# Two waiting lines for a sparse-attention and soft-MoE kernel's loads, and a step's second transposes ahead of its values

## The chip, the cores and the metric

The kernel runs on one core of one Trainium2 chip. The metric is the device time of one execution in microseconds. In the texts PE is the matrix engine (TensorE), PEld its weight loads, DVE the vector engine, ACT the scalar engine, POOL GpSimd, and SP the engine whose queue issues every DMA of this kernel.

## What is computed

The input is a batch of 8 with 8 heads of width 64, 512 local positions and 32 global ones. Everything is float32.

```python
s_g = scale * np.matmul(q_g, k_all.transpose(0, 1, 3, 2))      # 32 global queries see all 544 keys
out_g = np.matmul(sm(s_g), v_all)
s_ll = np.where(np.abs(pos[:, None] - pos[None, :]) <= 32, s_ll, -1e9)   # a local query: 65 neighbours
s_l = np.concatenate([s_lg, s_ll], axis=-1)                    # and the 32 global keys
out_l = np.matmul(sm(s_l), v_all)
x = concatenate([out_g, out_l]) laid out as (4352, 512)
logits = x @ phi                                               # 32 slots: 8 experts of 4
slot_input = softmax_over_rows(logits).T @ x
slot_out[e] = np.maximum(slot_input[e] @ w1[e], 0) @ w2[e]     # w1 512 x 1024, w2 1024 x 512
out = softmax_over_slots(logits) @ slot_out
```

## The kernel before

**Attention.** A unit u is four heads of one batch element, 16 units in all; it has three loads: k (704 KB), q (544 KB) and v (780 KB). Each unit is worked in two steps, so k counts 32 steps, with u = k // 2. The loop at L591 writes, for each step, in this order: the transposes of the shifted scores of step k-1 and their exponentials (transpose_exp, tiles t and pt), the parts run(k, "t"), the global queries of the next unit (make_qg, POOL, which reads the next q), the shift of the global scores (tile spg, POOL), the values of step k-2 (tile o), in odd steps the global values (tile og), the parts run(k, "b"), in even steps the transposes of the global scores (global_transpose, tile tg, exponential into ptg), the parts run(k, "c"), and then the scores of step k+1 (masks and scores, tile s, which read k and q) and their maximum and shift on DVE (tiles mx and sp). An even step closes with the global scores of its unit (tile g, copied into spg by ACT). make_v then copies pieces of v into va and vb on POOL, four copies a step, because the values read their windows of 128 keys from them.

The parts in "t", "b" and "c" are the first half of the mixture: "c" holds transposes of finished rows x (tile xt, in odd steps), "b" the logits (pl) and slot sums (pa), "t" the transposes of the exponentials (ptl).

**Order.** From L548 on the order of PE, DVE, ACT, POOL and SP is the order in which the code writes the work (manual_schedule), so each engine works through its own list, and an instruction that waits holds up those behind it. Transposes take one PSUM bank each from a ring of four (function bank): a group can start when the group four places before it has been read. The tiles o, g and the first scores share one other pair of banks (psV).

**Loads.** All loads go through SP's queue in order. The weights of the experts come in 64 pages of 512 KB (w); 30 of them have a place of their own and are loaded during the attention, two each unit. Four more take the places of the last k and q tiles. The rest follow when attention's buffers are given up (from L716 on). The loads of the attention are paced: matmul and transpose are wrapped (counted, L145) and count PE's instructions, and after every 253.75 of them release (L157) takes loads from the head of the list line, as long as the head fits in what is left of 10700 bytes a partition (GROUP; k takes 5632, q 4352, v 6240, a page 4096), and makes each wait for the PE instruction just written. need issues from the list without that wait, when a load that is needed next has not been issued. At the end of an even step the loop appends a page, k and q of unit u+2, and another page; v of unit u+1 goes to the head of the list in the odd step. The first loads (L538 to L546) and v of unit 1 are not paced.

## Time and profile before

| what | value |
|---|---|
| runs of the kernel before | 287.5 us median of 3 (286.36 to 287.97) |
| the profiled execution | 288.08 us, of it the span 286.3 us |
| mean granted clock of PE in it | 0.973 |
| DMA traffic | 77.05 MB, mean 269 GB/s |

The profile is of one execution. A row of its timeline gives the start in us from the span's start, the length, the engine, the line of the code, the operation, and output<-input by the names of the tiles; in brackets stands the idle time of the engine before it and who ended it. The chain of waits goes back from the last instruction to whatever released each step. "issue" as a releaser means that an engine waited for nothing that the profile shows. Line numbers are those of the kernel before; those of the changed kernel are larger by 1 to 5.

### The profile page before, as it was taken

The page shows a single profiled execution, that of the slowest core. Times are in us where ns is not written, and L with a number is a line of the kernel's source. Part 1 is how long each engine was busy: PE and PEld are TensorE (multiplying, and loading weights), DVE is VectorE, ACT ScalarE, POOL GpSimd, SP SyncE. Part 2 cuts the span into 40 slices and gives each one's busy share as a digit, 9 for nine tenths or more (in the row PEclk, how much of TensorE's full clock was granted, in tenths as well). Part 3 has the DMA queues.
Part 4 walks back from the last instruction along what each step waited for, and adds up shares of the span by engine and source line. Part 5 has one row for each costly group of instructions (what it writes and reads, how often), then busy time and mean ns, then how long its engine had stood idle before and what let it go on. Part 6 is the DMA issues. An engine that isn't in the chain of part 4 may idle for free.

```text
span 286.3 us, 14380 instructions
## 1 busy us (share of the span) xinstructions
PE 251.2 (88%) x6472; PEld 177.8 (62%) x6472; DVE 169.1 (59%) x360; ACT 120.9 (42%) x298; POOL 123.1 (43%) x182
## 2 busy tenths in 40 slices
PE   7749999899899986898999999899987999999920
PEld 4437777677677774676777877777765433655510
DVE  0744857576687856185678678577635764133730
ACT  1213464445546353344544555545473212124520
POOL 1077649557566673636465666466720000000000
PEclk9997999999999999799999999999999999999985
DMA  6964886867868875567576776878887999959998
GB/s 209 368 239 151 252 285 208 290 241 254 267 223 275 298 242 204 185 252 265 191 265 218 252 294 214 250 259 279 293 293 273 417 374 410 406 195 307 287 308 274
DMA packets 26909, 77.05 MB, mean 269 GB/s; under 512 B 2528, under 2 KB 12768, under 8 KB 26848
## 3 DMA queue, kind: packets, MB, share of 16 engines
q1 hardware_dynamic: 26848, 76.13, 76.2%
q8 instruction: 51, 0.84, 1.2%
q14 instruction: 10, 0.08, 0.1%
HBM read 67.21 MB, written 8.91 MB: 266 GB/s over the span
## 4 chain that ended last, share of the span: by engine, by line
PE 66%; DMA 15%; DVE 4%; issue 4%; SPq 2%; ACT 2%; POOL 2%; DVEq 0%; ACTq 0%; POOLq 0%
PE s L147 14%; DMA q<-in_qT_dram 12%; PE o L147 9%; PE t L147 8%; PE po L820 5%; PE g L147 5%; PE xt L147 4%; PE tg L147 4%; DMA v<-in_vS_dram 3%; PE pc L854 3%; PE pa L147 3%; PE ph L655 3%; PE pl L147 2%; PE og L147 2%; PE ht L670 1%
## 5 line engine op out<-in xcount | busy, mean ns | idle before, releaser
L261 DVE TENSOR_REDUCE mx<-s 128x8 f32<-128x1024 f32 x32 | 39.2, 1225 | 56.8 <-PE s L147 56.8
L147 PE MATMUL s<-k,q 64*32 64x128 f32 x2048 | 40.0, 281 | 9.0 <-DMA q<-in_qT_dram 4.8
L147 PEld LDWEIGHTS s<-k,q 64*32 64x32 f32 x2048 | 30.2, 108 | 21.3 <-issue 18.8
L272 ACT ACTIVATE pt<-t 128x512 f32<-128x512 f32 x64 | 34.9, 601 | 13.1 <-PE t L147 12.8
L263 DVE TENSOR_TENSOR sp<-s,mx 128x1024 f32<-128x1024 f32 x32 | 39.2, 1224 | 1.1
L215 POOL COPY va<-v 128x520 f32<-128x520 f32 (+1 forms) x32 | 23.2, 725 | 37.1 <-DMA v<-in_vS_dram 26.2
L147 PE MATMUL o<-v,pt 128*32 128x65 f32 x768 | 36.4, 221 | 1.7 <-issue 1.7
L147 PE MATMUL o<-va,pt 128*32 128x65 f32 x768 | 36.4, 221 | 0.2 <-POOL va L216 0.2
L147 PE MATMUL o<-vb,pt 128*32 128x65 f32 x512 | 35.3, 221 | 1.0 <-POOL vb L218 1.0
L147 PE MATMUL t<-con,sp 128*128 128x128 f32 x256 | 35.0, 280 | 0.0
L147 PEld LDWEIGHTS o<-v,pt 128*32 128x32 f32 x768 | 30.6, 109 | 4.7 <-issue 4.7
L147 PEld LDWEIGHTS o<-va,pt 128*32 128x32 f32 x768 | 30.6, 109 | 3.1 <-issue 2.2
L321 POOL TENSOR_SCALAR spg<-spg,m 128x640 f32<-128x640 f32 x16 | 30.1, 1883 | 2.0 <-DVE m L320 0.5
L147 PEld LDWEIGHTS o<-vb,pt 128*32 128x32 f32 x512 | 29.9, 110 | 1.2 <-POOL vb L218 1.2
L147 PEld LDWEIGHTS t<-con,sp 128*128 128x128 f32 x256 | 27.4, 141 | 5.1 <-issue 2.8
L384 ACT COPY xT<-xt 128x512 f32<-128x512 f32 x31 | 16.8, 588 | 32.2 <-PE xt L147 32.2
L316 ACT COPY spg<-g 128x640 f32<-128x640 f32 x16 | 11.1, 696 | 35.3 <-PE g L147 35.3
L224 POOL COPY qg<-q 64x64 f32<-64x64 f32 x32 | 7.4, 232 | 41.4 <-DMA q<-in_qT_dram 34.3
L297 DVE TENSOR_TENSOR xh<-o,r 128x256 f32<-128x256 f32 x64 | 24.2, 419 | 1.1
L216 POOL COPY va<-v 32x520 f32<-32x520 f32 (+1 forms) x32 | 23.0, 719 | 2.0
L147 PE MATMUL g<-k,qg 128*64 128x512 f32 (+2 forms) x192 | 21.8, 362 | 0.0
L346 ACT ACTIVATE xg<-og,rg 32x64 f32<-32x64 f32 x64 | 19.6, 306 | 4.6 <-DVE rg L342 1.9
(143 smaller groups left out, 399.1 us busy)
## 6 DMA issues: line engine op xcount, KB each, us to landing
w<-in_w_dram SPq DMA_DIRECT2D x64, 512.0 KB, 5.8
v<-in_vS_dram SPq DMA_DIRECT2D x16, 780.0 KB, 4.7
k<-in_kT_dram SPq DMA_DIRECT2D x15, 704.0 KB, 4.8
out_dram<-ob SPq DMA_DIRECT2D x32, 256.0 KB, 3.2
q<-in_qT_dram SPq DMA_DIRECT2D x15, 544.0 KB, 5.9
out_dram<-ob SPq DMA_DIRECT2D x8, 64.0 KB, 2.0
k<-in_kT_dram SPq DMA_DIRECT2D x1, 416.0 KB, 4.0
q<-in_qT_dram SPq DMA_DIRECT2D x1, 288.0 KB, 4.0
```

The costliest lines, as they stand in the source:

```text
L147: ins = emit(*args, **kw)
L215: nc.gpsimd.tensor_copy(va, v[:, m0:m1])
L216: nc.gpsimd.tensor_copy(va[0:32], v[0:32, m0 + 1:m1 + 1])
L261: nc.vector.tensor_reduce(mx, ps, axis=AX.X, op=ALU.max, negate=True)
L263: nc.vector.tensor_tensor(sps[k], ps, bc(mx, P), ALU.add)
L272: nc.scalar.activation(e[:, hh], pt, AF.Exp, scale=SCALE)
L297: nc.vector.tensor_tensor(xhs[u][:, 2 * a + t, :].rearrange("p (h d) -> p h d", h=4), po[:, t, :, 0:D], bc(r[:, t, :], D), ALU.mult)
L316: nc.scalar.copy(spg, pg[:, 0:640])
L321: later["shift"] = lambda: nc.gpsimd.tensor_scalar(spg, spg, m1, None, ALU.add)
L346: nc.scalar.mul(xgs[u // NU2][p0:p0 + 32, 256 * g + D * j:256 * g + D * j + D], po[32 * j:32 * j + 32, 0:D], r[32 * j:32 * j + 32])
L384: nc.scalar.copy(xT, pt)
L820: nc.tensor.matmul(po[h][32 * j:32 * j + 32, :], hTs[r][:, f, 32 * j:32 * j + 32], wt[1, 4 * r + j, h, f // 4][:, 256 * (f % 4):256 * (f % ...
```

## The change

Four things are done.

1. There are two lists. k, q and v stay in line, the pages go to fillers. release fills its room from line first, and from fillers with what is left. Both pages of a unit are appended at the end of the even step. What is left in fillers after the loop is issued there.
2. v of units 0 and 1 is no longer issued among the first loads: both wait in line and are released by PE's count.
3. In step 0 the two vb copies are made by ACT and not by POOL, and the shift of the first global scores is written ahead of make_v.
4. global_transpose and run(k, "c") stand right behind run(k, "t"), ahead of make_qg, of the shift and of the values.

```diff
--- before.py
+++ after.py
@@ -140,7 +140,7 @@
 
 
     count = [0, FIRST_BLOCK]
-    line = []
+    line, fillers = [], []
 
     def counted(emit, n):
         def f(*args, **kw):
@@ -156,16 +156,17 @@
 
     def release(ins):
         room = GROUP
-        while line and line[0][1] <= room:
-            room -= line[0][1]
-            issue(ins)
+        for q in (line, fillers):
+            while q and q[0][1] <= room:
+                room -= q[0][1]
+                issue(ins, q)
 
     def pace(load, ins):
         tc.add_manual_dep(load.ins, ins.ins.name,
                           mybir.DependencyInfo(mybir.DependencyClass.Sync, mybir.DependencyReason.DATA), reason="paced")
 
-    def issue(ins=None):
-        load = line.pop(0)[0]()
+    def issue(ins=None, q=None):
+        load = (line if q is None else q).pop(0)[0]()
         if ins is not None:
             pace(load, ins)
 
@@ -180,7 +181,7 @@
             resident[0] += 1
             return load_slot(resident[0] - 1)
 
-        line.append((load, 4096))
+        fillers.append((load, 4096))
 
     ks, qs, vs = {}, {}, {}
 
@@ -214,8 +215,9 @@
         vb = at.tile([P, 2, 4, VD], F32, tag=f"vb{a}", name=f"vb{k}")
         nc.gpsimd.tensor_copy(va, v[:, m0:m1])
         nc.gpsimd.tensor_copy(va[0:32], v[0:32, m0 + 1:m1 + 1])
-        nc.gpsimd.tensor_copy(vb[64:128], v[64:128, m0:m0 + 2])
-        nc.gpsimd.tensor_copy(vb[0:64], v[0:64, m0 + 1:m0 + 3])
+        copy = nc.gpsimd.tensor_copy if k else nc.scalar.copy
+        copy(vb[64:128], v[64:128, m0:m0 + 2])
+        copy(vb[0:64], v[0:64, m0 + 1:m0 + 3])
         vas[k], vbs[k] = va, vb
 
     def make_qg(u):
@@ -542,7 +544,7 @@
     nc.sync.dma_start(con, cst)
     load_k(1)
     load_q(1)
-    load_v(0)
+    line.append((lambda: load_v(0), 24 * VD * 4))
     nc.sync.dma_start(phisb, phi)
 
     order = tc.manual_schedule(engines={ENG.PE, ENG.DVE, ENG.Activation, ENG.Pool, ENG.SP})
@@ -594,6 +596,9 @@
         if k >= 1:
             transpose_exp(k - 1)
         run(k, "t")
+        if even and k >= 2:
+            global_transpose(u - 1)
+        run(k, "c")
         if not even and u + 1 < NU:
             need(qs, u + 1)
             make_qg(u + 1)
@@ -605,9 +610,6 @@
             if u + 1 < NU:
                 line.insert(0, (lambda u=u: load_v(u + 1), 24 * VD * 4))
         run(k, "b")
-        if even and k >= 2:
-            global_transpose(u - 1)
-        run(k, "c")
         run_later("global")
         if k + 1 < NH:
             need(ks, (k + 1) // 2)
@@ -622,12 +624,12 @@
         run(k, "e")
         run_later("totals")
         need(vs, u)
+        if k == 0:
+            run_later("shift")
         make_v(k)
         if even:
             if u == 0:
-                load_v(1)
-            if u < NU - 1:
-                page_later()
+                line.append((lambda: load_v(1), 24 * VD * 4))
             if u + 2 < NU:
                 line.append((lambda u=u: load_k(u + 2), 8 * KC))
                 line.append((lambda u=u: load_q(u + 2), 8 * QC))
@@ -636,6 +638,9 @@
                 line.append((lambda: borrow_slot(qp, "q", 2), 4096))
             if u < NU - 1:
                 page_later()
+                page_later()
+    while fillers:
+        issue(None, fillers)
     while line:
         issue()
     assert resident[0] == NWA
```

**SP's queue, units 2 to 4.** Before, from the second page on:

```order
L516 DMA w1_387<-in_w1_dram 128x1024
L516 DMA w2_485<-in_w1_dram 128x1024
L196 DMA k3_487<-in_kT_dram 128x1408
L204 DMA v2_583<-in_vS_dram 128x1560
L200 DMA q3_585<-in_qT_dram 128x1088
L516 DMA w3_691<-in_w1_dram 128x1024
L516 DMA w4_693<-in_w1_dram 128x1024
L204 DMA v3_783<-in_vS_dram 128x1560
L196 DMA k4_883<-in_kT_dram 128x1408
L200 DMA q4_885<-in_qT_dram 128x1088
```

After, from k of unit 2 on:

```order
L197 DMA k2_383<-in_kT_dram 128x1408
L201 DMA q2_385<-in_qT_dram 128x1088
L197 DMA k3_483<-in_kT_dram 128x1408
L201 DMA q3_485<-in_qT_dram 128x1088
L205 DMA v2_587<-in_vS_dram 128x1560
L518 DMA w1_589<-in_w1_dram 128x1024
L197 DMA k4_687<-in_kT_dram 128x1408
L201 DMA q4_689<-in_qT_dram 128x1088
L205 DMA v3_781<-in_vS_dram 128x1560
L518 DMA w2_783<-in_w1_dram 128x1024
```

The two pages between q of unit 2 and k of unit 3 have moved behind, and k and q of unit 4, which stood behind pages w3 and w4 and v of unit 3, now stand ahead of all three.

**PE, step 6 (an even step).** Before, from the last values of step 4 to the masks of step 7:

```order
L147 MATMUL o4_832<-v2_583,pt4_672 32x65 x2
L147 MATMUL o4_832<-va4_666,pt4_672 32x65
L147 MATMUL o4_832<-vb4_667,pt4_672 32x65
L147 MATMUL o4_832<-v2_583,pt4_672 32x65
L147 MATMUL tg2_128_871<-con_85,spg_96 128x128 x2
L147 MATMUL tg2_96_875<-con_85,spg_96 128x128 x3
L147 LDWEIGHTS mskt_86
L147 MATMUL s7_880<-mskt_86 128x4x96
```

After, from the step's first transposes on:

```order
L147 MATMUL t5_0_820<-con_85,sp5_652 128x128 x4
L147 MATMUL t5_1_826<-con_85,sp5_652 128x128 x4
L147 MATMUL tg2_128_832<-con_85,spg_96 128x128 x2
L147 MATMUL tg2_96_836<-con_85,spg_96 128x128 x3
L147 MATMUL o4_841<-v2_587,pt4_670 32x65 x2
L147 MATMUL o4_841<-va4_664,pt4_670 32x65
L147 MATMUL o4_841<-vb4_665,pt4_670 32x65
L147 MATMUL o4_841<-v2_587,pt4_670 32x65 x2
```

The two groups tg2 stood between the values o4 and the masks of s7; they now follow the groups t5 at once, and the values come behind them.

**ACT, the first steps.** Before, the first rows from the copy of the first global scores on:

```order
L316 COPY spg_96<-g0_218 128x640
L272 ACTIVATE pt0_236<-t0_0_237 128x512
L272 ACTIVATE pt0_236<-t0_1_243 128x512
L272 ACTIVATE pt1_301<-t1_0_302 128x512
L272 ACTIVATE pt1_301<-t1_1_308 128x512
L330 ACTIVATE ptg_97<-tg0_128_353 128x256
L330 ACTIVATE ptg_97<-tg0_96_357 96x384
```

After, from the same copy on:

```order
L318 COPY spg_96<-g0_218 128x640
L219 COPY vb0_230<-v0_187 64x520
L220 COPY vb0_230<-v0_187 64x520
L274 ACTIVATE pt0_235<-t0_0_236 128x512
L274 ACTIVATE pt0_235<-t0_1_242 128x512
L274 ACTIVATE pt1_299<-t1_0_300 128x512
L274 ACTIVATE pt1_299<-t1_1_306 128x512
L332 ACTIVATE ptg_97<-tg0_128_312 128x256
L332 ACTIVATE ptg_97<-tg0_96_316 96x384
```

The two copies of vb0, which read v of unit 0, now stand ahead of the exponentials pt0 of step 0; POOL's list loses them, and its shift of the first global scores stands ahead of va0.

## The prediction

> **What bounds the kernel now.** First the page's totals and the row of the small queue that carries no data of ours:

> ```profile
> span 286.3 us, 14380 instructions
> PE 251.2 (88%) x6472; PEld 177.8 (62%) x6472; DVE 169.1 (59%) x360; ACT 120.9 (42%) x298; POOL 123.1 (43%) x182
> q8 instruction: 51, 0.84, 1.2%
> ```

> PE is busy for 88% of the span, the next engine for 59%. So the question is where PE stands still. The waits of PE from 23 to 210 us, the attention after its start (total, times, longest):

> ```profile
> PE s L147 <- DMA q<-in_qT_dram: 4.4, 5, 1.4
> PE pa L147 <- issue: 4.1, 1, 4.1
> PE s L147 <- issue: 0.8, 1, 0.8
> PE o L147 <- issue: 0.4, 1, 0.4
> PE ptl L147 <- ACT dT L418: 0.3, 1, 0.3
> ```

> Only two rows are large: 4.4 us for five q loads, and one stop of 4.1 us that no semaphore explains. The same view for the first 23 us:

> ```profile
> PE tg L147 <- POOL spg L321: 1.3, 1, 1.3
> PE s L147 <- issue: 1.2, 1, 1.2
> PE o L147 <- POOL vb L218: 1.0, 1, 1.0
> ```

> The waits for vb and spg are POOL's and stand behind v of unit 0; what is left there are the first loads of k and q, which the change does not touch. Last, the granted clock in some stretches (PE busy first, the clock and DMA's share and rate at the end):

> ```profile
> 14.62:18.03 3.41, 2.01 (x29) 1.32 (x28) 1.89 (x2) 1.09 (x2) 1.83 (x3) 1.00 0.53 197
> 18.03:21.44 3.41, 1.34 (x60) 1.18 (x61) 1.68 (x5) 0.00 (x0) 3.22 (x6) 1.00 0.71 273
> 21.44:24.86 3.42, 3.42 (x73) 2.35 (x71) 0.00 (x0) 0.87 (x2) 3.18 (x6) 0.50 0.03 11
> 113.60:117.02 3.42, 1.14 (x17) 0.60 (x17) 0.01 (x1) 0.00 (x0) 2.72 (x4) 1.00 0.00 0
> 117.02:120.43 3.41, 3.41 (x51) 2.73 (x59) 0.74 (x1) 2.14 (x6) 2.46 (x4) 0.50 0.77 270
> ```

> Twice PE is busy for little of a stretch of 3.41 us (1.34 and 1.14), and in the next stretch it has half the clock: 1.7 us of work lost each time, if PE bounds there. So the stop of 4.1 costs 5.8.

> **The q loads, part by part.** Two places of the chain of waits, and the time of q's loads from issue to landing:

> ```profile
> 91.09 1.02 PE t L147 x8
> 92.11 1.06 PE o L147 x64
> 93.17 0.69 PE tg L147 x5
> 93.87 1.47 PE s L147 x66
> ...
> 95.66 5.61 DMA q<-in_qT_dram
> 101.40 1.15 PE s L147 x63
> 102.55 1.02 PE t L147 x8
> ...
> 111.20 0.57 PE og L147 x40
> 111.77 4.12 issue
> ```

> ```profile
> DMA to landing us min/median/max: 3.2/5.8/7.9
> ```

> This q is issued at 95.66, after the scores of one step, and wanted by the next scores, at 101.40 - one step later, 5.7 us for a load that takes 5.8. Each q that PE waits for stands so. In the new order k and q of unit 4 stand a page pair and a v earlier in SP's queue, and their release is written in step 5, for scores in step 7; before it was in step 6. A step lasts some 6 us (two lie between the t at 91.09 and the t at 102.55: 11.5). The load then has about 12 us for at most 7.9, so the 4.4 us go: **-4.4**. Their bounds: all stay, if loads released earlier land no earlier; nothing beyond 4.4 is to be had. The pages come later in turn, but nobody waits for a page before the tail, and both orders have issued 34 pages where the attention ends.

> **The start.** The first steps, with the price of a copy on ACT:

> ```profile
> 16.08 0.61 POOL L215 COPY va<-v 128x520 f32<-128x520 f32 x1 [8.35 <-DMA v<-in_vS_dram]
> 16.61 1.09 ACT L272 ACTIVATE pt<-t 128x512 f32<-128x512 f32 x2 [3.63 <-PE t L147]
> 18.09 0.61 POOL L218 COPY vb<-v 64x520 f32<-64x520 f32 x1
> 24.81 1.36 PE L147 MATMUL g<-k,qg 128*64 128x512 f32 x12
> ```

> ```profile
> L384 ACT COPY xT<-xt 128x512 f32<-128x512 f32 x31 | 16.8, 588 | 32.2 <-PE xt L147 32.2
> ```

> v of unit 0 lands just ahead of 16.08. Its load is now released during the second scores, a few us later, but it stood behind k and q of unit 1 in the queue anyway; I leave its landing at 16.0, and put half a microsecond on either side. From there ACT makes two copies (0.6 each, by its copy of 588 ns and POOL's 0.61): 17.3. Behind them in ACT's list stand the two exponentials of step 0, 1.09 together, which before were long done: 18.4. The new tg groups of step 2 take the banks of t of step 0, and so wait for these: their last transpose ends near 18.9 (five took 0.69). The values (1.06 and a seam) run until 20.2, masks and scores (1.47, with the seams 1.6) until 21.8, where the first g of unit 1 can start. POOL's two copies left (va, 0.61 each) end with ACT's, and the shift, written ahead of them, is done while v is awaited, so tg no longer waits for it. Before it started at 24.81: a gain of 3.0. This counts the full clock. PE has work for some 1.6 of the 3.41 us up to 18.03 (the 2.01 of its row less the first values in it), between the 1.34 that halved the clock and the 2.01 that did not; a halved stretch would take back up to 1.7.

> Then a new wait: k and q of unit 2 are both released by the scores at about 21, where k alone came at 16 before. Issued at 21.3, q lands 5.8 us on (the median above), at 27.1; PE wants it after g, t, o and og, (1.36, 1.02, 1.06, 0.57 and some 0.3 of seams and masks) at 26.1. Cost 1.0, between nothing and 2.5 (by the longest landing, 7.9, less a g that waits too). Start: 3.0 less 1.0, **-2.0**, from -3.2 to +1.2 (the full wait of 2.5 and the halved stretch).

> [...]

> **The stop of 4.1 us.** It begins behind og and lies 3 us behind the issue of a pair of k and q:

> ```profile
> 108.64 0.33 SPq L196 DMA_DIRECT2D k<-in_kT_dram  x1
> 109.02 0.42 SPq L200 DMA_DIRECT2D q<-in_qT_dram  x1
> ```

> The small queue moves 51 packets of 16 KB, PE's program by its size, and a packet that stands behind 1.25 MB of k and q comes late. This pair goes to another place of PE's program, and at the old one stands a page, 0.5 MB. I take it that the stop goes with its half clock: **-5.8**, between -5.8 and, if the new bursts of v with a page (1.3 MB) make one such stop more, +5.8.

> **The transposes.** The chain's rows show groups that follow one another to 0.01 us: 91.09 + 1.02 = 92.11, + 1.06 = 93.17, + 0.69 = 93.86. There is no seam to save, whichever group comes first; PE's work is 0. What changes is what they wait for. The moved groups issue no DMA, and POOL's order is the old one but in step 0. xt reads rows that a step before finished, and its two copies (0.59 each) now stand ahead of the global outputs on ACT, which is busy for 42%; the exponentials of tg stand ahead of those of the logits, whose transposes come a whole scores, g and t later (1.47 + 1.36 + 1.02). If ACT had not that room, the banks would come free late; in the attention PE now waits for it for 0.3 in all. tg now comes one group of values (1.06) earlier, and needs POOL's shift, which stands behind four copies of v and make_qg:

> ```profile
> 41.86 1.09 PE L147 MATMUL t<-con,sp 128*128 128x128 f32 x8
> 42.28 1.88 POOL L321 TENSOR_SCALAR spg<-spg,m 128x640 f32<-128x640 f32 x1
> 101.39 0.51 POOL L224 COPY qg<-q 64x64 f32<-64x64 f32 x2 [1.98 <-DMA q<-in_qT_dram]
> 101.99 1.89 POOL L321 TENSOR_SCALAR spg<-spg,m 128x640 f32<-128x640 f32 x1
> ```

> At 42 the shift ended at 44.16, 1.2 us behind the transposes' end at 42.95: tg would have waited that long. At 102 it ended at 103.88, and the transposes (102.55 + 1.02) at 103.57. But there make_qg stood idle for 1.98 us for the late q; with q early the shift is done by 102. So in most steps tg is safe by 1 to 2 us, and in the first few units it is not. g in turn comes nearer to the values whose bank it takes. For these new waits together, and for a short stop behind a burst, I put **+1.5**, between 0 and 6 (0.4 a step in 15 even steps).

> **The sum**, against the profiled execution's 288.08: 288.08 - 4.4 - 2.0 - 5.8 + 1.5 = **277.4**. That execution lies 0.6 above the median of the runs, 287.5, so it may hold a little more stopping than most.

> **Rivals.**

> *A stop of PE returns.* The new bursts of v and page are as long as k and q. For it: every unit has two bursts. Against: 1 of some 50 packets of program came so late. Time 277.4 + 5.8 = 283.2. Chance 0.2. [...]

> *POOL becomes the bound of the even steps.* v's load now stands right behind k and q in the queue. If it lands later by more than the margin of 1 to 2 us, the four copies (2.5 by 0.61 each), make_qg and the shift follow, and tg, and all of PE behind it, waits in each even step. As at 42 us, 1.2 in 15 steps is 18: 277.4 + 18 = 295.4. It outweighs the gains from 0.7 us a step on (0.7 x 15 = 10.5). Against it: v, the pair k and q, and the pages share a unit's 11.5 us in three releases, so v is released some 4 us behind q, whose transfer is then nearly done. Chance 0.06.

> *The tail keeps its end.* DMA's busy tenths over 40 slices of 7.2 us:

> ```profile
> DMA  6964886867868875567576776878887999959998
> ```

> From the 32nd slice on, near 222 us, it is at nine tenths for four slices, with the last pages. If these, and not PE, set the end, the attention's gain is lost: 288. Against it: their release hangs on PE's progress in the attention, so they move too. Chance 0.06.

> *Earlier releases, same landings.* SP's queue is in order, and a v that waits for its buffer holds k and q. Then only start and stop are gained: 277.4 + 4.4 = 281.8. Chance 0.08.

> **Chances.** The forecast has 0.6. Its own range is 273.5 (start -3.2, no new waits, and the small stops of 0.8 and 0.4 gone too: 288.08 - 3.2 - 4.4 - 5.8 - 1.2) to 281 (start +1.2 for -2.0). With the first and last rival it reaches 284; that leaves out 0.12 above and a little below. A measurement of this kernel tells a change from about 0.5%, so from 286.06: faster 0.6 + 0.2 + 0.08 = 0.88, same 0.06 (the tail), slower 0.06 (POOL).

> **What would show it.** PE's waits from 23 to 210 us without q, the first g of unit 1 near 22, a wait for q of unit 2 near 26. The stop: no row of PE behind "issue" over 2 us, no stretch at half clock near 117. The rival on POOL: PE tg behind spg with more than 5 us in total. I am wrong if the q rows are gone and the time has not fallen by 8 or more.

## The result, and the profile after

The changed kernel takes 301.45 us (median of 4 runs, 298.06 to 302.07), the kernel before 287.74 beside it (286.36 to 291.37). The ratio is 1.0469, with a 95% interval from 1.0364 to 1.0575: slower, where 277.4 was forecast. (Here and below the medians are over all runs; the ratios leave out runs that were disturbed, of either kernel, and are missing where too few were left.) The profiled execution took 300.98 us, 12.9 more than that of before.

The page of the changed kernel, the rows that answer to those of before; behind the group of the scores s stands PE's idle time just before them:

```profile
span 299.2 us, 14395 instructions
PE 255.5 (85%) x6472; PEld 179.3 (60%) x6472; DVE 170.3 (57%) x360; ACT 119.6 (40%) x300; POOL 121.5 (41%) x180
q8 instruction: 51, 0.84, 1.1%
PE 75%; issue 8%; DMA 6%; DVE 3%; ACT 2%; POOL 1%; SPq 1%; DVEq 0%; ACTq 0%; POOLq 0%
L147 PE MATMUL s<-k,q 64*32 64x128 f32 x2048 | 42.5, 276 | 13.8 <-issue 11.0
```

PE has the same 6472 matmuls, no other engine is busy for over 1.2 us more, and yet the span is 12.9 us longer. The row of shares is that of the chain that ended last: 8% of it is now "issue", time for which the profile shows no releaser; before it was 4%. PE's waits from 23 to 210 us (total, times, longest):

```profile
PE s L147 <- issue: 10.3, 10, 3.5
PE o L147 <- issue: 4.1, 3, 1.7
PE s L147 <- DMA q<-in_qT_dram: 1.4, 1, 1.4
PE og L147 <- issue: 1.2, 2, 0.8
PE xt L147 <- issue: 0.5, 1, 0.5
PE pl L147 <- issue: 0.4, 1, 0.4
PE tg L147 <- POOL spg L323: 0.4, 1, 0.4
```

None of the five late loads of q is left (4.4 us before). The one row on q is another wait, the one that the prediction expected for q of unit 2 near 26 us:

```profile
23.61 0.38 SPq L201 DMA_DIRECT2D q<-in_qT_dram  x1
29.14 0.43 PE L147 MATMUL s<-k,q 64*32 64x128 f32 x13 [1.39 <-DMA q<-in_qT_dram]
```

But the rows behind "issue", which summed to 5.3 us before (4.1 + 0.8 + 0.4), sum to 16.5 now (10.3 + 4.1 + 1.2 + 0.5 + 0.4), in 17 stops instead of three.

The start: first two of PE's waits up to 23 us, then rows of the timeline on ACT and PE.

```profile
PE tg L147 <- POOL qg L226: 1.9, 1, 1.9
PE s L147 <- issue: 1.4, 2, 1.0
```

```profile
16.65 0.62 ACT L219 COPY vb<-v 64x520 f32<-64x520 f32 x1 [3.79 <-DMA v<-in_vS_dram]
22.72 0.66 PE L147 MATMUL s<-k,q 64*32 64x128 f32 x30 [0.98 <-issue]
23.32 1.36 PE L147 MATMUL g<-k,qg 128*64 128x512 f32 x12
```

g of unit 1 starts at 23.32 where it started at 24.81. v landed 0.6 later than the forecast's 16.0, and a stop of 0.98 without a releaser stands in the scores just ahead of g. The wait of tg, 1.9 us until 18.54, is put down to POOL's qg, which tg does not read. tg reads spg, whose shift was done at 16.14, and takes the bank of the first transposes of step 0, whose exponential on ACT ended at 18.40: it is the wait for ACT that the prediction has in its sum.

Where the rest of the time went is seen at the longest stop. The chain of waits there:

```profile
130.59 0.98 PE s L147 x20
131.57 3.55 issue
135.12 0.92 PE s L147 x46
```

SP's queue at that time:

```profile
127.69 0.33 SPq L197 DMA_DIRECT2D k<-in_kT_dram  x1
128.10 0.38 SPq L201 DMA_DIRECT2D q<-in_qT_dram  x1
131.54 0.33 SPq L205 DMA_DIRECT2D v<-in_vS_dram  x1
131.92 0.43 SPq L518 DMA_DIRECT2D w<-in_w_dram  x1
```

And four stretches of 3.40 us (PE busy first, the granted clock, DMA's share and rate last):

```profile
126.20:129.60 3.40, 2.85 (x68) 2.42 (x68) 2.04 (x3) 2.75 (x5) 3.14 (x6) 1.00 0.27 61
129.60:133.00 3.40, 1.97 (x92) 1.29 (x80) 1.35 (x6) 1.04 (x4) 3.22 (x4) 1.00 1.00 357
133.00:136.40 3.40, 1.28 (x50) 1.08 (x51) 0.30 (x1) 0.19 (x1) 0.61 (x1) 1.00 0.85 334
136.40:139.80 3.40, 3.40 (x32) 3.07 (x33) 2.15 (x2) 1.96 (x4) 0.00 (x0) 0.50 0.06 25
```

PE stops in the middle of a group of 66 scores whose inputs are all there. v and a page, 1292 KB, were issued only 0.03 us before, so they cannot have caused the stop: by the sizes of the packets in the trace (5632 and 4352 bytes, k's and q's), what fills DMA from 128.6 to 132.6 is k and q, issued at 127.69 and 128.10. The packet of q8 that belongs here starts at 132.6, when they run out, 4.95 us behind the issue of k, and ends at 133.6; PE goes on 1.5 us later, at 135.12. At the stop of 4.1 us before, the packet also started 4.95 us behind the issue of k (108.64 and 113.59). The stretch with 1.28 us of work is followed by one at half clock (0.50), as at 1.34 and 1.14 before. By these rows the stop cost 3.55 us, and the half clock behind it an estimated 1.7, half of its stretch of 3.40.

The account of the 12.9 us goes by g of the last unit, before and after:

```profile
201.24 1.36 PE L147 MATMUL g<-k,qg 128*64 128x512 f32 x12
210.65 1.36 PE L147 MATMUL g<-k,qg 128*64 128x512 f32 x12
```

It starts 9.4 later. Of these the stops are +11.2 (16.5 less 5.3), the late loads of q -4.4, the start -0.1 (g of unit 1 1.5 earlier, the new wait for q 1.4), together 6.7. The other 2.7 are put down to no row; the busy time of all 2048 scores went from 40.0 to 42.5. Behind that point it is 3.5 more: among it a stretch at half clock from 228.5 on, 1.7, and stops without a releaser of 2.1 and 1.0 ahead of xtg and og, where before had one of 1.3.

### The profile page after: what moved, and what is told of

It is laid out like the page before. It is cut to its first block, busy times and chain, and to the rows that moved or that the text cites. A ratio compares the mean times of both kernels' runs of the same rounds, so it can differ in the third digit from the quotient of the medians.

```text
span 299.2 us, 14395 instructions
## 1 busy us (share of the span) xinstructions
PE 255.5 (85%) x6472; PEld 179.3 (60%) x6472; DVE 170.3 (57%) x360; ACT 119.6 (40%) x300; POOL 121.5 (41%) x180
## 4 chain that ended last, share of the span: by engine, by line
PE 75%; issue 8%; DMA 6%; DVE 3%; ACT 2%; POOL 1%; SPq 1%; DVEq 0%; ACTq 0%; POOLq 0%
PE s L147 16%; PE o L147 11%; PE t L147 9%; PE g L147 6%; PE xt L147 5%; PE po L825 5%; PE tg L147 3%; PE og L147 3%; PE pc L859 3%; PE ph L660 3%; PE pa L147 3%; PE pl L147 2%; DMA v<-in_vS_dram 2%; DMA k<-in_kT_dram 2%; DMA q<-in_qT_dram 2%
## 5 line engine op out<-in xcount | busy, mean ns | idle before, releaser
L147 PE MATMUL s<-k,q 64*32 64x128 f32 x2048 | 42.5, 276 | 13.8 <-issue 11.0
L147 PEld LDWEIGHTS s<-k,q 64*32 64x32 f32 x2048 | 30.1, 106 | 27.1 <-issue 25.3
L147 PE MATMUL o<-v,pt 128*32 128x65 f32 x768 | 37.0, 222 | 2.8 <-issue 2.8
L147 PE MATMUL o<-vb,pt 128*32 128x65 f32 x512 | 36.1, 222 | 1.7 <-issue 1.7
L147 PE MATMUL o<-va,pt 128*32 128x65 f32 x768 | 36.5, 222 | 0.0
L147 PE MATMUL t<-con,sp 128*128 128x128 f32 x256 | 35.5, 282 | 0.0
L147 PEld LDWEIGHTS o<-va,pt 128*32 128x32 f32 x768 | 30.7, 110 | 5.1 <-issue 4.9
L318 ACT COPY spg<-g 128x640 f32<-128x640 f32 x16 | 11.1, 696 | 56.4 <-PE g L147 56.4
L147 PEld LDWEIGHTS o<-v,pt 128*32 128x32 f32 x768 | 31.1, 110 | 3.7 <-issue 3.7
L147 PEld LDWEIGHTS t<-con,sp 128*128 128x128 f32 x256 | 27.8, 142 | 6.2 <-ACT xg L348 2.4
L147 PEld LDWEIGHTS o<-vb,pt 128*32 128x32 f32 x512 | 30.2, 110 | 1.9 <-issue 1.9
L296 DVE TENSOR_SCALAR r<-o 128x8 f32<-128x8 f32 x32 | 5.3, 167 | 32.7 <-PE o L147 32.6
L147 PE MATMUL g<-k,qg 128*64 128x32 f32 (+2 forms) x192 | 22.2, 362 | 0.0
L219 POOL COPY vb<-v 64x520 f32<-64x520 f32 x31 | 19.2, 619 | 1.6
```

The source lines that it names most:

```text
L147: ins = emit(*args, **kw)
L219: copy(vb[64:128], v[64:128, m0:m0 + 2])
L318: nc.scalar.copy(spg, pg[:, 0:640])
```

## The experiments

The program's packets are the thing to watch: 51 of 16 KB, and PE's compiled list, the list of instructions that the compiler makes for PE, has 13036 of them in the changed kernel, 256 to a packet (13036 in 51). That list holds the matmuls, the weight loads and also instructions that only wait for a semaphore: 101 of these before, 87 in the changed kernel. The transposes, moved up, need 14 waits fewer. The kernel's count sees the matmuls with their weight loads, but not the waits, so 253.75 was a guess at 256 less the waits. With 14 fewer, the releases slide back through the blocks: their place (the number of the releasing instruction, modulo 256, counted in the compiled list) went from 203 to 187 over the attention before, and goes from 201 to 173 now. "Place" below is this number, and a "burst" is a group of loads that one release issues.

The traces say what the stops are. In all 20 kept traces together PE has 209 stops of over 0.3 us without a releaser between 23 us and g of the last unit. Counted in the trace with the waits, PE had run at each of them 256 instructions for every packet of q8 landed by its end, and 193 or 194 more, so each lies at the same place of a block; and PE goes on 1.2 to 1.6 us behind the end of a packet (0.8 once). So I read these stops as PE standing at the end of what has been fetched. In the numbering of "place" that border is at 194 or 195.

The theories: **place** (a burst released too early in a block is in the queues ahead of the packet with the next instructions, and PE runs dry), **order of the groups** (the moved transposes, 5 of tg in 0.69 us and 8 of xt in 1.02 in e17, used to separate the short matmuls, 64 of the values in 1.06; more than 256 short instructions in a row now outrun the fetching), **bytes** (the bursts are simply too long or too much), and **POOL** (tg now waits for the shift). The kernel before itself had medians from 288.5 to 293.3 in the five groups of runs that follow, so each is compared with the runs of before beside it.

**Both orders of loads, with and without the move, and two places.** e1 is the changed kernel with the place held, e2 is the kernel before with the drift of the changed one, e3 is the changed kernel without the fourth part of the change, e4 is the kernel before with that part alone.

e1, place 201 to 208:

```diff
-FIRST_BLOCK, BLOCK, GROUP = 200, 253.75, 10700
+FIRST_BLOCK, BLOCK, GROUP = 200, 254.4, 10700
```

e2, place 203 to 173:

```diff
-FIRST_BLOCK, BLOCK, GROUP = 200, 253.75, 10700
+FIRST_BLOCK, BLOCK, GROUP = 200, 253.4, 10700
```

e3, place 201 to 186 (e4 is the same edit the other way round, in the kernel before; place 203 to 173):

```diff
         run(k, "t")
-        if even and k >= 2:
-            global_transpose(u - 1)
-        run(k, "c")
...
         run(k, "b")
+        if even and k >= 2:
+            global_transpose(u - 1)
+        run(k, "c")
```

e1: 

> The changed kernel with one number altered: a release every 254.4 counted instructions in place of 253.75. In the changed program PE's list holds 14 fewer waiting instructions than before (87 for 101), which the count does not see, so that a release falls ever earlier within a block of 256 instructions (from place 201 of the block to 174; before from 203 to 188). With 254.4 it stays between 201 and 208. Theory 1, the place of the release within the block: a release that comes early puts its loads ahead of PE's next 16 KB of program, PE stops for them; with 254.4 the stops without a releaser fall from some 20 us to under 8, and the time to 275 to 283. Theory 2, the larger bursts of two lists (v with a page, 1.3 MB): the place plays no part, 297 to 303. Theory 3, the transposes' own waits: 297 to 303 too.

e2: 

> The kernel before with a release every 253.4 counted instructions in place of 253.75: nothing but the places of the releases moves, from 203 to 173 within the block of 256, much as in the changed kernel. Theory 1: slower, 293 to 303, with more and longer stops of PE without a releaser. Theories 2 and 3: 286 to 290, as before.

e3: 

> The changed kernel without the move of the transposes: two lists, paced v loads, the copies on ACT, and both groups of transposes where they stood before. PE's list has 100 waiting instructions, the releases go from place 201 to 186. Theory 1: most of the loss is gone, 276 to 286. Theory 2: the loss stays, 296 to 303. Theory 3: the loss is gone, 275 to 285; this run does not part theories 1 and 3.

e4: 

> The kernel before with the move of the transposes alone: one list, all loads as before. 87 waiting instructions on PE, releases from place 203 to 173. Theory 1: slower than before, 293 to 303, much as the run that only alters the count. Theory 2: as before, 286 to 290. Theory 3: 293 to 303, but with PE's waits named after POOL, DVE or ACT and not without a releaser.

Before beside them: 288.49. e1: 291.21, ratio 1.0126 [0.9995, 1.0257]. e2: 302.60 (292.02 to 310.0). e3: 288.70, ratio 0.9996 [0.9908, 1.0084]. e4: 306.63, ratio 1.0661 [1.0507, 1.0814]. So the lists, the later v and the copies on ACT cost nothing (e3), but gain nothing that shows in the time either, though q is early there too; the move alone, at +6.6%, costs about what the whole change costs, 4.7% (e4; the intervals overlap). In e4 a part of it is not the place: tg waits 4.4 us for POOL's shift at the start, 1.3 before, as the shift is not written ahead of make_v there. A slide of the place alone, with nothing moved, makes the median 14 us longer (e2; its runs are too far apart for a ratio, the lowest is 292.02). Holding the place takes most of the loss back (e1), but misses its expectation of 275 to 283: its rows behind "issue" still sum to 10.7 us up to 204.

**Other places and sizes.** e5 releases later in the block, e6 makes the bursts shorter (no v with a page), e7 holds the place in the kernel before, e8 holds it without the move and with short bursts.

Each changes the one line of the constants, here in the order e5 (place 224 to 232), e6 (as e1), e7 (201 to 206), e8:

```diff
-FIRST_BLOCK, BLOCK, GROUP = 200, 253.75, 10700
+FIRST_BLOCK, BLOCK, GROUP = 224, 254.4, 10700
+FIRST_BLOCK, BLOCK, GROUP = 200, 254.4, 10000
+FIRST_BLOCK, BLOCK, GROUP = 200, 254.1, 10700
+FIRST_BLOCK, BLOCK, GROUP = 200, 254.1, 10000
```

e5: 

> The changed kernel with the first release at 224 counted instructions in place of 200 and one every 254.4: every release stands at places 224 to 232 of its block of 256, 24 instructions behind the run with 254.4 alone. Theory 1 (the loads of a release must not get ahead of PE's next 16 KB of program): the program is then fetched ahead of each burst, stops without a releaser fall under 5 us, time 274 to 284. Theory 2 (the size of a burst, v with a page, decides, wherever it is released): 289 to 296, as with 254.4 alone.

e6: 

> The changed kernel with 254.4 and a room of 10000 bytes a partition in place of 10700: k with q still fits (9984), v with a page (10336) does not, so v goes alone and the pages go two at a time, as before. Some five pages more are left for the end of the attention. Theory 2: the stops behind v with a page (about 1 us a unit) go, attention ends 8 to 12 us earlier than with 254.4 alone, time 279 to 286. Theory 1: places are the same as with 254.4 alone, 288 to 294.

e7: 

> The kernel before with a release every 254.1 counted instructions, which holds the place at 201 to 206 of the block throughout (before it drifts from 203 to 187). Theory 1: the one stop of 4.1 us and most of the late packets of program are gone, 280 to 286. Theory 2: as before, 286 to 290.

e8: 

> Two lists, paced v loads and ACT's copies without the move of the transposes, a release every 254.1 (places 200 to 205) and a room of 10000 (v alone, pages two at a time). It has what I forecast to gain, early k and q and the faster start, without the bursts of v and page and without the drift. Theory 1 and 2 both: 274 to 282. If it stays at 286 to 290, the early k and q are worth nothing by themselves, and my sum's largest term was wrong for another reason.

Before beside them: 293.33. e5: 297.13 (288.48 to 299.13, and one run of 791.79 that I cannot explain). e6: 292.23, ratio 1.0227 [1.0085, 1.037]. e7: 291.63, ratio 1.0045 [0.9841, 1.0248]. e8: 294.35, with runs from 279.11 to 299.21. e5, e7 and e8 miss what the theory of the place expected of them, e6 comes out as it expected. There is no sign that later is better than 200 to 208 (e5 has no ratio), nor that shorter bursts take away what e1 left; the kernel before gains nothing that can be measured from a held place. e8 decided nothing: its spread is wider than the question. Its one run of 279.11 shows only that a time near the forecast can occur.

**The move alone with the place held, and without the pages.** e11 issues all 30 pages behind the attention; the computation is complete.

e9 is e4 with blocks of 254.4 (place 200 to 208), e10 the changed kernel once more, e12 e1 once more. e11:

```diff
-        for q in (line, fillers):
+        for q in (line,):
```

e9: 

> The kernel before with the move of the transposes alone, and a release every 254.4, which holds the place at 200 to 208 of the block of 256. The move alone with 253.75 (places 203 down to 173) took 306.6 us median against 288.5. Theory 1, the place of the release: with the place held the loss goes, within 2% of the kernel before. Theory 4, the order of the groups itself makes PE's program run dry, wherever the loads are released: 300 or more again.

e10: 

> The changed kernel as it is, once more, so that it stands on the same chip beside the next kernel: 298 to 303 by its first runs. Every theory.

e11: 

> The changed kernel with no page released during the attention: all 30 pages are issued behind it, so the whole is longer, and what counts is the time of the last global scores (g of unit 15, at 210.7 us in the changed kernel, 201.2 before). Only k, q and v move, at the changed kernel's early places. If PE's program is late because data stands ahead of it in the DMA engines, fewer bytes (2.1 in place of 3.1 MB a unit) take most stops away: 188 to 196, stops without a releaser under 6 us. If the stops come from PE's program itself, 205 or more.

e12: 

> The changed kernel with a release every 254.4 again, on the chip of the changed kernel itself. Theory 1: 2 to 5% under the changed kernel in the same call, and within 2% of the kernel before. Theory 4: as the changed kernel.

Before beside them: 292.01. e9: 297.62, ratio 1.0316 [1.0251, 1.0381]. e10: 298.44, ratio 1.0275 [1.017, 1.038]. e11: 324.68, as its pages come late; for the attention, g of the last unit starts at 202.7, against 210.7 in the changed kernel's first profile (188 to 196 was expected). e12: 293.88, without a ratio. The changed kernel's loss is smaller beside these runs than at first, 2.7% for 4.7%. The held place takes the move alone from +6.6% to +3.2%, and of these 3.2% a part is again tg's wait for POOL at the start, 4.9 us in e9. A third of the bytes less in the attention shortens it by 8.0, holding the place alone by 7.4 (203.3 in e1); stops without a releaser stay (8.4 us ahead of the scores in e11). So bytes have a part in it, but are not all of it.

**Without the move, the drift; with the place held, half the move.** e14 keeps the whole move, but puts the odd steps' t behind run(k, "b"), so that slow transposes stand between the sums and the scores again.

e13 is e3 with blocks of 253.4 (place 201 to 174). e14, with blocks of 254.4:

```diff
-        if k >= 1:
+        if k >= 1 and even:
             transpose_exp(k - 1)
...
         run(k, "b")
+        if not even:
+            transpose_exp(k - 1)
```

e15, with blocks of 254.4 (e16, with blocks of 254.1, moves the two lines of global_transpose in the same way, and leaves run(k, "c")):

```diff
-        run(k, "c")
...
         run(k, "b")
+        run(k, "c")
```

e13: 

> The changed kernel without the move of the transposes, with blocks of 253.4: the place of the releases within PE's 256 instructions drifts from 201 to 174, as it does in the changed kernel (201 to 173), where without the move and at 253.75 it drifted only to 186. Theory 'place': the drift alone carries the cost, so the time is near the changed kernel's 298 to 301, PE's stops behind no releaser sum to 12 us or more between 23 and 205 us, and g of unit 15 starts at 208 or later. Theory 'order of the groups': without the move the stops stay few, the time is within 1% of the kernel without the move (288.7) and g of unit 15 starts before 200. Both at work: 291 to 296.

e14: 

> The changed kernel with blocks of 254.4 (place held at 201 to 205) in which the odd steps' transposes t stand behind the logits and sums, directly ahead of the masks and scores, so that the short matmuls of values, global values and sums (about 240) are again cut off from those of the scores (136) by slow ones. The even steps are left as the change has them. Theory 'order of the groups' (over 256 short matmuls in a row outrun the fetching of the program): the cost left with the place held (291 to 294) falls by about half or more, to 287 to 290, and the odd steps' stops of the scores go. Theory 'bursts alone': no gain, 291 to 295. Rival: the t groups now stand later than their readers want them and ACT's exponentials end later, which PE would show as values waiting for ACT pt; then 295 or more.

e15: 

> The changed kernel with the place held (254.4, 201 to 206), but only the transposes tg of the even steps are moved; xt of the odd steps stand behind the sums again. Theory 'order of the groups': the even steps then run values, logits and scores in a row (192 + 136 = 328 short matmuls), the odd steps do not; about half of the remaining cost: 289 to 292. If tg's earlier wait for POOL's shift is what costs, PE's tg behind spg shows over 2 us and the time is that of both moves, 291 to 294.

e16: 

> The changed kernel with the place held (254.1, 201 to 207), but only the transposes xt of the odd steps are moved; tg of the even steps stand ahead of the masks again. Theory 'order of the groups': the odd steps run values, global values, sums and scores in a row (240 + 136 = 376 short matmuls), which is the longer of the two stretches: at least half of the remaining cost, 289 to 293, with the stops in the odd steps. If tg's earlier wait is what costs, the time is that of the kernel without the move, 286 to 289.

Before beside them: 292.25. e13: 302.23, ratio 1.0333 [1.02, 1.0466], g of the last unit at 212.8. Without any move, the slide to 174 alone makes a loss of the size of the changed kernel's. Its place falls below the border of 194 at some 72 us. PE's rows behind "issue" sum to 0.5 us from 23 to 72, and to 19.5 from there to 213. In the changed kernel the place falls below it at some 85 us: of its stops over 0.3 us, 2.9 us lie ahead of that, 12.6 behind. Releases just behind the border are not free of stops, though: before's own of 4.1 us followed a release at 195, and with the place held e1, e14 and e15 still have 10.7, 11.1 and 12.1 us of rows behind "issue". e14: 291.42, ratio 0.9913 [0.9812, 1.0014]. e15: 292.02, ratio 0.9883 [0.9644, 1.0123]. e16: 292.86, ratio 1.0192 [1.012, 1.0264]. By the ratios what is left with the place held comes with xt and not with tg, and POOL is out of it (e15 has tg's earlier wait, 0.4 us behind spg, and no loss). That e14, with xt and tg both moved, is faster than e16, with xt alone, speaks for the long row of short matmuls with their weight loads (240 instructions of the values, global values and sums, then some 130 of masks and scores). Neither is shown: the medians of the three, 291.42, 292.02 and 292.86, lie 1.5 us apart, e15's ratio rests on two of its runs, and one profile of each does not tell them apart (e14 11.1 us of stops behind "issue", e16 8.9).

**The place itself, or that it slides.** Both without the move; e17 holds the place at 201 to 204, e18 at 177 to 180.

In both the constants of e3 are changed, first e17, then e18:

```diff
-FIRST_BLOCK, BLOCK, GROUP = 200, 253.75, 10700
+FIRST_BLOCK, BLOCK, GROUP = 200, 254.1, 10700
+FIRST_BLOCK, BLOCK, GROUP = 176, 254.1, 10700
```

e17: 

> The changed kernel without the move, with blocks of 254.1 from 200 on: every release lies at 201 to 204 of PE's 256 instructions. Theory 'place': at least as fast as with the drift to 186 (288.7) and 8 us or more faster than with the drift to 174 (302.2): 283 to 289, with g of unit 15 before 198. If the drift costs by itself and not the place, the same. A rival, that only the early blocks matter: 288 to 292.

e18: 

> The same kernel with blocks of 254.1 from 176 on: every release lies at 177 to 180, all through the attention, with no drift. Theory 'place': all blocks now have the place that the drift reaches only near the end (174), so it is as slow as the drift or slower: 300 to 312, with more than 12 us of PE's stops behind no releaser. Rival 'only a steady place is wanted': as e17, 283 to 290.

Before beside them: 290.75 (287.55 to 294.7). e17: 286.58 (281.82 to 290.25), ratio 0.9789 [0.9707, 0.9872]: 1.3 to 2.9% faster than the kernel before, though the runs of the two overlap. e18: 318.80 (299.44 to 324.15), the slowest of all but e11, by one constant that differs by 24. Its lowest run lies above every run of e17 and of before beside them. e17 has g of the last unit at 201.0, where before 198 was expected, and e18 is slower than its 300 to 312. PE's waits in e17 from 23 to 205 us:

```profile
PE s L147 <- issue: 2.4, 3, 1.5
PE pa L147 <- issue: 2.3, 1, 2.3
PE s L147 <- DMA q<-in_qT_dram: 2.2, 1, 2.2
PE pl L147 <- issue: 1.4, 2, 0.8
PE o L147 <- issue: 1.1, 2, 0.7
PE og L147 <- issue: 0.7, 2, 0.5
...
PE tg L147 <- issue: 0.3, 1, 0.3
```

The same in e18, up to 240 us, since its attention is longer:

```profile
PE s L147 <- issue: 16.1, 8, 3.0
PE o L147 <- issue: 7.8, 8, 2.0
PE og L147 <- issue: 4.7, 3, 2.5
PE tg L147 <- issue: 2.4, 1, 2.4
PE g L147 <- issue: 1.9, 1, 1.9
PE pl L147 <- issue: 1.6, 2, 1.1
PE t L147 <- issue: 1.4, 2, 0.9
PE pa L147 <- issue: 1.2, 1, 1.2
```

The rows behind "issue" sum to 8.2 us in e17 and to 37.1 in e18. e17's releases lie behind the border, e18's ahead of it. One stop of e18 shows the course of it from end to end. SP's queue, where the second page of the row "x2" was issued at the end of its 5.50:

```profile
75.03 0.33 SPq L205 DMA_DIRECT2D v<-in_vS_dram  x1
75.41 5.50 SPq L518 DMA_DIRECT2D w<-in_w_dram  x2
```

The chain of waits:

```profile
79.65 0.90 PE s L147 x27
80.55 2.04 issue
82.59 0.86 PE s L147 x39
```

Busy times in two stretches (PE first; clock, DMA's share and rate last):

```profile
75.00:80.00 5.00, 3.77 (x110) 2.95 (x118) 2.98 (x5) 2.44 (x7) 0.61 (x1) 1.00 0.73 264
80.00:81.00 1.00, 0.55 (x25) 0.28 (x26) 0.51 (x2) 0.24 (x1) 0.89 (x2) 1.00 0.07 20
```

v and the page keep DMA busy until 80. The packet of q8 starts only then, at 80.2, 5.2 us behind the issue of v, with the engines nearly empty (0.07, 20 GB/s), and ends at 81.2. PE has run dry at 80.55 and goes on at 82.59, 1.4 us after the packet. In e17 the burst of the same kind:

```profile
82.33 0.33 SPq L205 DMA_DIRECT2D v<-in_vS_dram  x1
82.72 3.50 SPq L518 DMA_DIRECT2D w<-in_w_dram  x2
```

```profile
82.93 0.87 PE pl L147 x32
83.80 0.69 PE tg L147 x5
84.50 1.59 PE s L147 x66
```

Here the packet starts at 83.0, 0.7 us behind the issue of v, as k and q issued ahead of it run out and before v's own data come, and PE has no stop. Over all packets between 23 and 205 us, the start of each less the last issue of a load ahead of it is, in the median: before 0.50, e17 0.42, e3 0.52, changed kernel 1.40, e18 3.89 us; over 1.5 us lie 6 of 41, 10 of 41, 8 of 41, 19 of 39 and 25 of 34. The times follow, roughly: a packet can also stand behind an earlier burst than the last, as in the changed kernel's longest stop, and that this figure does not see. When a packet is asked for no trace shows; that this is near the border is my estimate from where the releases hurt (stops of 8.2 us at 201 to 204, 37.1 at 177 to 180).

## Why the prediction was wrong, point by point

- **The q loads, -4.4.** Right: the five waits are gone. That this much did not come off the time is due to the other terms; e3, with q as early and no move, is no faster than before (0.9996).
- **The start, -2.0.** g of unit 1 came 1.5 earlier instead of 3.0: v landed 0.6 later than set, and a stop of 0.98 stood in the scores. The wait for q of unit 2 came as set, 1.4 for 1.0, so the term came out at about -0.1, within its range. The half clock that the range allowed for did not come. In the kernel before the stretch from 21.44 to 24.86 ran at half clock (1.7 us of work); in the changed one no stretch does from 6.7 to 136.4, and the gain of 1.5 is no more than that.
- **The stop of 4.1 us, "I take it that the stop goes with its half clock: -5.8".** This is the step that failed. The stop at 111.77 is gone, but 17 stops stand in the place of three: 11.2 us more than before instead of 5.8 less, with a stretch at half clock still there (from 136.4 now). That is 17.0 of the 23.6 us between 277.4 and the profiled 300.98. The cause named, the program's packet behind a burst, was the right one, and e17 against e18 and e3 against e13 show it. What was wrong was to treat the place as a matter of one pair, and chance. Each release has its place in a block of 256, set by a count that does not see waiting instructions, and the change shifted all of them.
- **The transposes: "PE's work is 0".** True of its matmuls and blind to its list: 14 waiting instructions fewer move the places from 187 to 173 at the end. Nothing in the working counted instructions that do nothing. e13 (the slide without the move) shows that this is enough for the loss. What is left of the move's cost with the place held, 0 to 3% in e1, e9 and e16, is not explained: it may come with xt (e16), where a longer row of short matmuls stands; that this row is the cause was not shown.
- **The new waits, +1.5.** tg behind spg is 0.4; the sum of such rows is below the forecast. With it the rival on POOL, the one that was put forward as the slower end, falls: tg waits for next to nothing behind the start, and e15 has it without a loss.
- **"A stop of PE returns", 283.2 at a chance of 0.2.** The right cause at a third of its size: it was priced as one more stop, 5.8 over the sum, where 17.0 came. The row it was weighed by, one late packet of some 50, is what the places of before, 187 and up, made of it; in the changed kernel 19 of 39 start over 1.5 us behind the last issue of a load. The rows behind "issue" sum to 8.2 us at place 201 to 204 (e17) and to 37.1 at 177 to 180 (e18).
- **The tail** was not its own bound, it moved with PE; it grew by 3.5, with two more stops and a half clock in it.

## What to carry to other kernels

Where loads are released by an engine's progress, ask at which place of that engine's program they go out, counted in its compiled list with the instructions that only wait: a reordering that adds no work can change that number for everything behind it, as it did here (14 such instructions fewer, and 173 for 187 at the end). Rows behind "issue" in the middle of a group, close behind a large burst, were the sign here (3.55 us inside a group of 66 scores, behind 1.25 MB of k and q); before such a kernel is judged, its places are to be set again (e17 against e18: 286.6 and 318.8 us for 24 instructions). The border was read from the stops themselves: all 209 lie 193 or 194 instructions past the 256 for each packet landed. And a gain of some us that is read off waits is worth nothing until the stops without a releaser have a cause and a bound of their own.
